# Halving the first layer norm's row sums, moving a later one to ScalarE, and cutting the last store in two on a kernel that keeps TensorE busy

## The chip, the cores and the metric

One core of a Trainium2 chip. The metric is the device time of one launch in microseconds (us). The kernel runs at the full granted TensorE clock (1.00). Below, PE is TensorE, DVE is VectorE, ACT is ScalarE, SP is SyncE; SPq and ACTq are the queues from which SyncE and ScalarE issue transfers.

## The reference, cut to what matters

Two layers, each an attention part A and a gated part B, on one sequence of 2048 tokens with 1024 features, in bf16:

```python
x = x + A(layernorm(x), wqkv, wo)      # qkv = ln @ wqkv; 32 heads; a window of 8 keys at stride 2; then @ wo
x = x + B(layernorm(x), w1, w3, w2)    # (silu(ln @ w1) * (ln @ w3)) @ w2, inner size 3584
x = x + A(layernorm(x), wqkv, wo)
x = x + B(layernorm(x), w1, w3, w2)
```

The layer norm has no learnt scale: (x - mean) / sqrt(var + 1e-5) for each token.

## The kernel before

The program is written as a list of operations with the keys that they read and write. A small scheduler in the kernel file then places them by modelled times and emits every engine's instructions in that order. So an edit of one operation can move instructions of other engines. Tokens are handled in four chunks of 512, each of four tiles of 128 tokens.

**The head.** To start matmuls early, the first two token tiles are only centred, not scaled. Their row sums are made like this: tile 0 by halves on two engines, tile 1 whole on ScalarE. PE transposes the centred tiles (through `ident`), the transposes are evacuated to `ce`, and PE multiplies them by the rows of the query weights as these rows land:

```python
dve(0.77, ... tensor_scalar(xn[2][:, 0:512], x_sb[0][:, 0:512], 1.0 / D, 0.0, ..., accum_out=mean[:, 0:1]), ...)
act(0.82, ... activation(xn[3][:, 0:512], x_sb[0][:, 512:1024], ACTF.Copy, scale=1.0 / D, accum_out=part[:, 0:1]), ...)
act(1.25, ... activation(xn[3][:], x_sb[1][:], ACTF.Copy, scale=1.0 / D, accum_out=mean[:, 1:2]), ...)
for j in range(2):
    for h in range(2):
        ... # dve: xn[j] half h = x_sb[j] half h - mean
    transposed(xn[j], ..., ce[:, :, j * P:(j + 1) * P], ..., pieces of the evacuation)
...
for kk, j0, j1 in [(k, j, j + 1) for j in range(2) for k in range(3)] + [(k, 0, 2) for k in range(3, KT)]:
    ...  # 8 matmuls: weight row kk times tiles j0 to j1; reads ("w", row kk) and ("ce", j, kk)
```

After these come 64 matmuls of 256 columns for tiles 2 and 3, and then the key product and everything else with 512 columns.

**The last chunk's layer norm** before its query, key and value products uses DVE's statistics instructions, two of 512 columns and one aggregate for each of the four tiles:

```python
for j in range(TPC):
    stats(j)
root(0, TPC)
```

**The tail.** The very last matmul group is 128 columns wide; DVE adds it to x and the result is stored from one queue:

```python
evac(dve, ..., tensor_tensor(xs, xs, bank[a.bank][:, 0:cn], op=ALU.add), ...)
if l == 1:
    dma(cn // 4, xout[:, n, hh * 512 + c0:hh * 512 + c0 + cn], xs, [("x", n, hh)], [("out", n, hh)], 0)
```

## Time and profile before

| | before |
|---|---|
| time, median of 5 runs | 1614.94 us (1614.66 to 1615.42) |
| span in the profiled run | 1613.1 us |
| PE / DVE / ACT busy | 1601.3 / 1122.3 / 329.6 us |
| start of the first 512-column matmul | 21.49 us |
| from there to the end of the last add | 1589.16 us |
| from the last add to the end of the span | 2.48 us |

The page of the kernel before: its span, the busy times with their shares and instruction counts, and the chain that ended last by engine.

```profile
span 1613.1 us, 19082 instructions
PE 1601.3 (99%) x7463; PEld 762.7 (47%) x7610; DVE 1122.3 (70%) x1906; ACT 329.6 (20%) x526; POOL 5.3 (0%) x28
PE 99%; issue 1%; DMA 0%; ACT 0%; DVE 0%; ACTq 0%
```

The Trainium skill ("Trainium Kernel Development and Optimization", Performance Expectations) warns that matmul busy time is a bad metric of how close a kernel is to its limit, because matmuls are pipelined. A busy share alone would not show where time can be gained, so look at the waits. The wait view of PE in the kernel before (engine and line, what it waited for, us in total, times, longest) lists these three and no more:

```profile
PE bank L285 <- PEq L757: 0.8, 1, 0.8
PE bank L430 <- DVE xn L472: 0.4, 1, 0.4
PE bank L521 <- DMA slot<-in_A_wqkv_dram: 0.2, 1, 0.2
```

All three lie before 7 us. Between 21.49 us and its last matmul PE waits for nothing that the view lists, and then only the last add follows: this stretch is 1589.16 us of matmuls. The windows view of exactly that stretch (us from the start, its length, busy us and instructions of each engine, granted clock, DMA share, GB/s):

```profile
21.49:1610.65 1589.16, 1581.09 (x7271) 746.74 (x7416) 1112.98 (x1878) 317.16 (x501) 0.00 (x0) 1.00 0.59 176
```

What can be gained is therefore in the first 21.5 us and the last 2.5. The timeline of PE at the head (start, duration, line, operation, count, and in brackets the idle time before it and what ended it):

```profile
5.19 0.61 PE L521 MATMUL bank<-hT,slot 128*128 128x128 bf16 x8
5.96 0.62 PE L521 MATMUL bank<-hT,slot 128*128 128x128 bf16 x8 [0.16 <-DMA slot<-in_A_wqkv_dram]
6.96 0.66 PE L430 MATMUL bank<-ident,xn 128*128 128x128 bf16 x8 [0.39 <-DVE xn L472]
7.46 5.44 PE L521 MATMUL bank<-hT,slot 128*128 128x128 bf16 x64
...
14.51 1.69 PE L535 MATMUL bank<-xnT,slot 128*128 128x256 bf16 x14
```

L521 is the product with the query weights (the first two lines are weight rows 0 and 1 for tile 0), the L430 line is the transposes of tile 1, and L535 begins the 256-column matmuls. PE stands idle 0.39 us until DVE has centred tile 1. What DVE waits for there, in the timeline of DVE and ACT:

```profile
5.37 1.06 ACT L460 ACTIVATE xn<-x 128x1024 bf16<-128x1024 bf16 x1 [1.35 <-DMA x<-in_A_x_dram]
6.33 0.19 ACT L460 ACTIVATION_READ_ACCUMULATOR xn<-x 128x1 f32 x1
6.55 0.62 DVE L472 TENSOR_SCALAR xn<-x,mean 128x512 bf16<-128x512 bf16 x2 [1.22 <-ACT xn L460]
```

The tail, in the timeline of the kernel before: the last add, and the issue of the last store.

```profile
1610.36 0.29 DVE L700 TENSOR_TENSOR x<-x,bank 128x128 bf16<-128x128 bf16 x1 [1.27 <-PE bank L347]
1610.68 0.33 SPq L261 DMA_DIRECT2D out_dram<-x  x1
```

### The profile page before, as it was taken

The page shows a single profiled execution, that of the slowest core. Times are in us where ns is not written, and L with a number is a line of the kernel's source. Part 1 is how long each engine was busy: PE and PEld are TensorE (multiplying, and loading weights), DVE is VectorE, ACT ScalarE, POOL GpSimd, SP SyncE. Part 2 cuts the span into 40 slices and gives each one's busy share as a digit, 9 for nine tenths or more (in the row PEclk, how much of TensorE's full clock was granted, in tenths as well). Part 3 has the DMA queues.
Part 4 walks back from the last instruction along what each step waited for, and adds up shares of the span by engine and source line. Part 5 has one row for each costly group of instructions (what it writes and reads, how often), then busy time and mean ns, then how long its engine had stood idle before and what let it go on. Part 6 is the DMA issues. An engine that isn't in the chain of part 4 may idle for free.

```text
span 1613.1 us, 19082 instructions
## 1 busy us (share of the span) xinstructions
PE 1601.3 (99%) x7463; PEld 762.7 (47%) x7610; DVE 1122.3 (70%) x1906; ACT 329.6 (20%) x526; POOL 5.3 (0%) x28
## 2 busy tenths in 40 slices
PE   9999999999999999999999999999999999999999
PEld 7555544444444444444444444444444444444444
DVE  5899888988889888898898729884299831211211
ACT  5423322021201222113311032110321101101110
POOL 1000000000000000000000000000000000000000
PEclk9999999999999999999999999999999999999999
DMA  9834755495548764858545487365873464454451
GB/s 321 228 105 151 221 166 171 127 227 158 171 141 253 194 186 137 216 164 251 176 131 163 157 248 228 121 176 174 254 220 118 160 179 156 144 177 149 156 167 42
DMA packets 350649, 285.80 MB, mean 177 GB/s; under 512 B 72288, under 2 KB 344928, under 8 KB 350560
## 3 DMA queue, kind: packets, MB, share of 16 engines
q1 hardware_dynamic: 350128, 283.94, 58.8%
q8 instruction: 59, 0.97, 0.2%
q10 hardware_dynamic: 432, 0.66, 0.1%
q14 instruction: 30, 0.25, 0.1%
HBM read 238.94 MB, written 29.36 MB: 166 GB/s over the span
## 4 chain that ended last, share of the span: by engine, by line
PE 99%; issue 1%; DMA 0%; ACT 0%; DVE 0%; ACTq 0%
PE bank L347 98%; PE bank L535 0%; PE bank L521 0%; DMA x<-in_A_x_dram 0%; PE bank L430 0%; ACT L281 0%; DVE xn L472 0%; ACT xn L460 0%; DVE x L700 0%; ACTq L460 0%
## 5 line engine op out<-in xcount | busy, mean ns | idle before, releaser
L347 PE MATMUL bank<-xnT,slot 128*128 128x512 bf16 x4955 | 1088.7, 379 | 5.3
L347 PEld LDWEIGHTS <-slot 128*128 128x128 bf16 x5056 | 518.2, 102 | 572.9
L347 PE MATMUL bank<-slot,hT 128*128 128x512 bf16 (+2 forms) x1812 | 387.3, 372 | 1.9
L670 DVE TENSOR_TENSOR hT<-sg,bank 128x512 bf16<-128x512 bf16 x224 | 153.4, 685 | 214.4 <-PE bank L347 194.9
L265 DVE TENSOR_TENSOR scr<-scr 128x1024 bf16<-128x1024 bf16 (+3 forms) x576 | 293.4, 539 | 2.0
L347 PEld LDWEIGHTS <-hT 128*128 128x128 bf16 x1848 | 178.5, 98 | 208.7
L668 ACT ACTIVATE sg<-bank 128x512 bf16<-128x512 f32 x224 | 133.7, 597 | 660.5 <-PE bank L347 608.8
L265 DVE TENSOR_TENSOR scr<-qT,kT 128x2048 bf16<-128x2048 bf16 x128 | 154.1, 1219 | 73.3 <-DMA kT<-qkv_d 71.0
L405 ACT CAST sgt<-bank 128x512 bf16<-128x512 f32 x184 | 107.3, 585 | 315.2 <-PE bank L347 300.3
L265 DVE TENSOR_TENSOR scr<-pA,vT 128x2048 bf16<-128x2048 bf16 x128 | 152.5, 1220 | 0.3
L700 DVE TENSOR_TENSOR x<-x,bank 128x512 bf16<-128x512 bf16 (+1 forms) x66 | 43.9, 670 | 121.5 <-PE bank L347 121.4
L347 PE MATMUL bank<-wo,oT 128*128 128x512 bf16 x502 | 112.6, 379 | 0.6
L313 DVE BATCH_NORM_STATS2 st<-x 128x6 f32<-128x512 bf16 x124 | 81.8, 681 | 11.9 <-DMA x<-in_A_x_dram 11.4
L347 PEld LDWEIGHTS <-oT 128*128 128x128 bf16 x512 | 50.1, 98 | 60.3
L645 DVE TENSOR_TENSOR x<-x,bank 128x512 bf16<-128x512 bf16 x64 | 43.9, 687 | 37.0 <-PE bank L347 35.8
L320 ACT ACTIVATE sd<-mv,epst 128x4 f32<-128x4 f32 (+1 forms) x17 | 5.1, 297 | 172.4 <-DVE mv L316 172.1
L628 DVE STREAM_TRANSPOSE pA<-pB 128x2048 bf16<-128x2048 bf16 x16 | 37.0, 2310 | 0.5
L605 DVE STREAM_TRANSPOSE pB<-pA 128x2048 bf16<-128x2048 bf16 x16 | 37.0, 2310 | 0.5
L668 ACT ACT_TABLE_LOAD x20 | 25.7, 1283 | 56.2 <-PE bank L347 56.0
L265 DVE TENSOR_TENSOR pA<-scr 128x256 bf16<-128x256 bf16 x128 | 35.9, 286 | 0.4
L265 DVE TENSOR_TENSOR oT<-scr 128x256 bf16<-128x256 bf16 x128 | 33.9, 288 | 0.1
L327 DVE TENSOR_SCALAR xn<-x,mv,rstd 128x1024 bf16<-128x1024 bf16 x62 | 30.7, 541 | 3.5 <-DMA xnT<-xn 3.4
(61 smaller groups left out, 209.0 us busy)
## 6 DMA issues: line engine op xcount, KB each, us to landing
slot<-in_B_w_dram SPq DMA_DIRECT2D x160, 1024.0 KB, 5.9
slot<-in_A_wqkv_dram SPq DMA_DIRECT2D x28, 1024.0 KB, 5.1
qkv_d<-sgt SPq DMA_DIRECT2D x92, 256.0 KB, 3.3
qT<-qkv_d SPq DMA_DIRECT2D x16, 512.0 KB, 5.7
slot<-in_B_w_dram SPq DMA_DIRECT2D x16, 512.0 KB, 5.7
kT<-qkv_d SPq DMA_DIRECT2D x14, 544.0 KB, 6.7
vT<-qkv_d SPq DMA_DIRECT2D x14, 544.0 KB, 4.9
out_dram<-x SPq DMA_DIRECT2D x31, 128.0 KB, 4.3
```

The costliest lines, as they stand in the source:

```text
L265: return lambda _: nc.vector.tensor_tensor(o, a, b, op=op)
L313: dve(0.67, lambda _, hh=hh: nc.vector.bn_stats(st[q][:, j, hh, :], x_sb[n][:, hh * 512:(hh + 1) * 512]), [("x", n, hh)] + list(after), [( ...
L320: act(0.3, lambda _: nc.scalar.activation(sd[q][:, j0:j1], mv[q][:, j0:j1, 1], ACTF.Sqrt, bias=epst[:]), [("mv", q, j) for j in range(j0, ...
L327: dve(0.5, lambda _: nc.vector.tensor_scalar(xn[j][:], x_sb[n][:], mv[q][:, j, 0:1], rstd[q][:, j:j + 1], op0=ALU.subtract, op1=ALU.mult), ...
L347: nc.tensor.matmul(bank[a.bank][:, 0:ncol], lhsT=w, rhs=r, start=first and i == 0, stop=last and i == n - 1)
L405: evac(act, 0.59, lambda _, a=a, i=i, m=m: nc.scalar.copy(sgt[i][:, m % 2, :], bank[a.bank][:]), op, [], [("sgt", i, m % 2)], a)
L605: dve(2.31, lambda _: nc.vector.transpose(psmT[:].rearrange("p c d -> p (c d)"), psm[:].rearrange("p w s -> p (w s)")), allA, ["pB"])
L628: dve(2.31, lambda _: nc.vector.transpose(At[:].rearrange("p w s -> p (w s)"), AeT[:].rearrange("p c d -> p (c d)")), ["pB"], allA)
L645: evac(dve, t1(512), lambda _, xs=xs, a=a: nc.vector.tensor_tensor(xs, xs, bank[a.bank][:], op=ALU.add), op, [("x", n, hh)], [("x", n, hh) ...
L668: evac(act, 0.6, lambda _, i=i, a=ag: nc.scalar.activation(sg[i][:], bank[a.bank][:], ACTF.Silu), og, [], [("sg", i)], ag, table="silu")
L670: evac(dve, t1(512), lambda _, i=i, a=au, f=f: nc.vector.tensor_tensor(hT[:, f, :], sg[i][:], bank[a.bank][:], op=ALU.mult), ou, [("sg", i ...
L700: evac(dve, t1(cn), lambda _, xs=xs, a=a, cn=cn: nc.vector.tensor_tensor(xs, xs, bank[a.bank][:, 0:cn], op=ALU.add), op, [("x", n, hh)], [ ...
```

## The change

The intent is to shorten both ends. Tile 1's row sum is made by halves on two engines as tile 0's is; its sum of squares moves behind the evacuations on ScalarE; the last chunk's sums go to ScalarE, which has more room than DVE; the output weights `wo` come in four loads, not five; and the last store leaves as two halves of 64 partitions (rows), on two queues at once.

```diff
+        def sums(j):      # Copy with scale 1/D, then Square with bias mean, scale -1, each with accum_out
+            act(1.25, ... ACTF.Copy, scale=1.0 / D, accum_out=mv[q][:, j, 0:1] ...)
+            act(1.35, ... ACTF.Square, bias=mv[q][:, j, 0:1], scale=-1.0, accum_out=mv[q][:, j, 1:2] ...)
...
-            stats(j)
-        root(0, TPC)
+            if on_act:    # l == 0 and c == NCH - 1
+                sums(j)
+            else:
+                stats(j)
+        root(0, TPC, D if on_act else 1)
...
-        act(1.25, lambda _: nc.scalar.activation(xn[3][:], x_sb[1][:], ACTF.Copy, scale=1.0 / D,
-                                                 accum_out=mean[:, 1:2]), ...)
         for j in range(2):
+            dve(0.77, ... xn[2][:, 0:512], x_sb[j][:, 0:512] ... accum_out=mean[:, j:j + 1]),
+                [("x", j, 0)] + [("ce", 0, 2)] * j, ...)
+            act(0.82, ... xn[3][:, 0:512], x_sb[j][:, 512:1024] ... accum_out=part[:, j:j + 1]), ...)
...
-                       ((0, 2, "DVE"), (2, 4, "DVE"), (4, 8, "ACT")) if j == 0 else ((0, 4, "DVE"), (4, 8, "ACT")))
+                       ((0, 2, "DVE"), (2, 4, "DVE"), (4, 8, "ACT")))
...
-                [("x", j, 0), ("x", j, 1), ("mean", j)] + [("ce", 1, KT - 1)],
+                [("x", j, 0), ("x", j, 1), ("mean", j), ("xnT", b, 3, 1) if j else ("ce", 1, KT - 1)],
...
-        for t0, t1_ in ((0, 2), (2, 4), (4, 6), (6, 7), (7, 8)):
+        for t0, t1_ in ((0, 2), (2, 4), (4, 6), (6, 8)):
...
-                    dma(cn // 4, xout[:, n, hh * 512 + c0:hh * 512 + c0 + cn], xs, [("x", n, hh)], [("out", n, hh)], 0)
+                    parts = ((0, 64, "SP"), (64, P, "AQ")) if pi == len(pieces) - 1 and tail else ((0, P, "SP"),)
+                    for p0, p1, queue in parts:
+                        dma(cn * (p1 - p0) // 512, xout[p0:p1, n, hh * 512 + c0:hh * 512 + c0 + cn], xs[p0:p1],
+                            [("x", n, hh)], [("out", n, hh, p0)], 0, queue=queue)
```

Because the scheduler sees other durations, PE's order changed too: weight row 2's eight matmuls for tile 0 now stand before the transposes of tile 1 instead of after them. I call these the new and the old order.

More of the change, by code (lines that the diff above doesn't have):

```diff
@@ L302, with ln @@
     stage_no = [0]
-    def ln(c, first=False):
+    def ln(c, first=False, on_act=False):
         s = stage_no[0]
@@ L317, in stats, with root @@
                 [("st", q, j, 0), ("st", q, j, 1)], [("mv", q, j)], pri)
-        def root(j0, j1):
-            act(0.3, lambda _: nc.scalar.activation(sd[q][:, j0:j1], mv[q][:, j0:j1, 1], ACTF.Sqrt, bias=epst[:]),
+        def sums(j):
+            xt = x_sb[c * TPC + j]
+            keys = [("x", c * TPC + j, hh) for hh in range(2)]
+            act(1.25, lambda _: nc.scalar.activation(xn[j][:], xt[:], ACTF.Copy, scale=1.0 / D,
+                                                     accum_out=mv[q][:, j, 0:1]), keys, [("xn", j), ("mv", q, j)], 1)
+            act(1.35, lambda _: nc.scalar.activation(xn[j][:], xt[:], ACTF.Square, bias=mv[q][:, j, 0:1], scale=-1.0,
+                                                     accum_out=mv[q][:, j, 1:2]), keys, [("xn", j), ("mv", q, j)], 1)
+        def root(j0, j1, n=1):
+            act(0.3, lambda _: nc.scalar.activation(sd[q][:, j0:j1], mv[q][:, j0:j1, 1], ACTF.Sqrt, bias=epst[:],
+                                                    scale=1.0 / n),
                 [("mv", q, j) for j in range(j0, j1)] + ["eps"], [("sd", q, j) for j in range(j0, j1)], -9 if first else 0, table="sqrt")
@@ L413, in q_stage @@
     def q_stage(l, c):
-        b = ln(c)
+        b = ln(c, on_act=l == 0 and c == NCH - 1)
         for which in range(3):
@@ L453, in q_first @@
         ce = hT[:, 8:16, :]
-        dve(0.77, lambda _: nc.vector.tensor_scalar(xn[2][:, 0:512], x_sb[0][:, 0:512], 1.0 / D, 0.0, op0=ALU.mult,
-                                                    op1=ALU.add, accum_out=mean[:, 0:1]),
-            [("x", 0, 0)], [("xn", 2), ("mean", 0)], -9)
-        act(0.82, lambda _: nc.scalar.activation(xn[3][:, 0:512], x_sb[0][:, 512:1024], ACTF.Copy, scale=1.0 / D,
-                                                 accum_out=part[:, 0:1]), [("x", 0, 1)], [("xn", 3), ("part", 0)], -9)
@@ L459, in q_first @@
-        rows[2](6, queue="AQ", after=[("part", 0)])
-        act(1.25, lambda _: nc.scalar.activation(xn[3][:], x_sb[1][:], ACTF.Copy, scale=1.0 / D,
-                                                 accum_out=mean[:, 1:2]), [("x", 1, 0), ("x", 1, 1)],
-            [("xn", 3), ("mean", 1)], -9)
-        for j in range(2):
-            for h in range(2):
-                c0 = 512 * h
-                if j == 0:
-                    dve(0.31, lambda _, c0=c0: nc.vector.tensor_scalar(
-                        xn[0][:, c0:c0 + 512], x_sb[0][:, c0:c0 + 512], mean[:, 0:1], part[:, 0:1], op0=ALU.subtract,
-                        op1=ALU.subtract), [("x", 0, 0), ("x", 0, 1), ("mean", 0), ("part", 0)],
-                        [("xn", 0), ("xn", 0, h)], -9)
-                else:
-                    dve(0.31, lambda _, c0=c0: nc.vector.tensor_scalar(
-                        xn[1][:, c0:c0 + 512], x_sb[1][:, c0:c0 + 512], mean[:, 1:2], None, op0=ALU.subtract),
-                        [("x", 1, 0), ("x", 1, 1), ("mean", 1)], [("xn", 1), ("xn", 1, h)], -9)
+        for j in range(2):
+            dve(0.77, lambda _, j=j: nc.vector.tensor_scalar(xn[2][:, 0:512], x_sb[j][:, 0:512], 1.0 / D, 0.0,
+                                                             op0=ALU.mult, op1=ALU.add, accum_out=mean[:, j:j + 1]),
+                [("x", j, 0)] + [("ce", 0, 2)] * j, [("xn", 2), ("mean", j)], -9)
+            act(0.82, lambda _, j=j: nc.scalar.activation(xn[3][:, 0:512], x_sb[j][:, 512:1024], ACTF.Copy,
+                                                          scale=1.0 / D, accum_out=part[:, j:j + 1]),
+                [("x", j, 1)], [("xn", 3), ("part", j)], -9)
+            if j == 0:
+                rows[2](6, queue="AQ", after=[("part", 0)])
+            for h in range(2):
+                dve(0.31, lambda _, j=j, c0=512 * h: nc.vector.tensor_scalar(
+                    xn[j][:, c0:c0 + 512], x_sb[j][:, c0:c0 + 512], mean[:, j:j + 1], part[:, j:j + 1],
+                    op0=ALU.subtract, op1=ALU.subtract), [("x", j, 0), ("x", j, 1), ("mean", j), ("part", j)],
+                    [("xn", j), ("xn", j, h)], -9)
@@ L475, in q_first @@
             transposed(xn[j], [("xn", j, h) for h in range(2)], ce[:, :, j * P:(j + 1) * P],
                        [("ce", j, k) for k in range(KT)],
-                       ((0, 2, "DVE"), (2, 4, "DVE"), (4, 8, "ACT")) if j == 0 else ((0, 4, "DVE"), (4, 8, "ACT")))
-        dve(0.16, lambda _: nc.vector.tensor_tensor(mean[:, 0:1], mean[:, 0:1], part[:, 0:1], op=ALU.add),
-            [("mean", 0), ("part", 0), ("ce", 1, 0)], [("mean", 0)], -9)
+                       ((0, 2, "DVE"), (2, 4, "DVE"), (4, 8, "ACT")))
@@ L480, in q_first @@
+        dve(0.16, lambda _: nc.vector.tensor_tensor(mean[:], mean[:], part[:], op=ALU.add),
+            [("mean", j) for j in range(2)] + [("part", j) for j in range(2)] + [("ce", 1, 0)],
+            [("mean", j) for j in range(2)], -9)
         for j in range(2, TPC):
@@ L642, in t_stage @@
                 op = mm8(a, [(oT[oh][:, t, j * P:(j + 1) * P], wo[:, t, hh * 512:(hh + 1) * 512]) for t in range(KT)],
-                         True, True, [("oT", oh, t) for t in range(KT)] + [("wo", t) for t in (0, 2, 4, 6, 7)], lane=1)
+                         True, True, [("oT", oh, t) for t in range(KT)] + [("wo", t) for t in (0, 2, 4, 6)], lane=1)
                 xs = x_sb[n][:, hh * 512:(hh + 1) * 512]
```

## The prediction

> **What bounds the kernel.** TensorE. The page gives PE 1601.3 us busy of a 1613.1 us span, at full granted clock; the chain of waits is 99% PE. Matmuls run every 0.216 us (the chain's pieces, 49 in 10.74 us; the 0.05 us breaks between pieces look like lost records). The wait view gives PE three short waits after its warm-up, all before 7 us, and none until its last matmul at 1610.34. So only the first 22 us and the last 2.8 us can give anything; DVE (70% busy) and ScalarE (20%) are off the path. The Trainium skill warns ("Trainium Kernel Development and Optimization", Performance Expectations) that matmul busy time is a bad metric; I rely on the constant interval and the missing waits.
>
> **What the change moves.**
>
> 1. *Token tile 1 by halves.* Before (timeline): x tile 1 lands at 5.33; ScalarE sums its 1024 columns in 1.06 + 0.19 us; DVE subtracts from 6.55; PE starts the transposes at 6.96. After: two 512-column sums side by side (DVE 0.61 + 0.08, ScalarE 0.63 + 0.19) make the centred tile ready about 0.3 us earlier. But the instruction order shows PE doing weight row 2's eight matmuls for tile 0 before these transposes, and row 2 lands at about 6.6. PE then transposes from about 7.1 and starts tile 1's products at about 7.65 instead of 8.06: 0.4 us. The gain then shrinks: DVE now writes normalised tile 0 (0.53 us) before it evacuates the transposes of tiles 2 and 3, so the 256-column matmuls that began at 14.67 begin at about 14.4. Weight rows land just in time (row 5 about 10.7).
> 2. *Tile 1's squares later on ScalarE* (1.15 + 0.19 us). Its DMA transpose is issued at about 17.3 instead of 14.9; undisturbed ones of this trace land in 3.1 to 3.4 us, so at 20.6, before the K products need it at 21.2. Tight; I expect no stall.
> 3. *Last chunk's sums on ScalarE.* About 6.3 us off DVE (eight statistics of 0.68, four aggregates of 0.2), about 10.3 us onto ScalarE. Neither is on the path: 0.
> 4. *wo in four loads, not five*: 0.
> 5. *Last store.* Before: last add ends 1610.65, issue 0.33 us, packets 1611.56 to 1611.83, landed 1612.17, closing barrier to 1613.1. Issue took 0.33 us for 128 rows of 256 or 512 bytes alike, so half the rows hardly shorten it. The skill ("DMA: Bandwidth & Descriptors", Issuing engines are not separate DMA queues) says several issuers share the same 16 engines and save only issue time. Gain 0 to 0.1.
>
> **Sum.** About 0.25 us at the head and 0.05 at the tail: 1614.94 becomes 1614.6 us. The 8-in-10 range is 1614.0 to 1615.3, as the runs before already spread over 0.6. Chances: faster by over 2% 0.003, within 2% 0.99, slower by over 2% 0.007.
>
> **What would show it.** Timeline: tile 1's transposes at about 7.1, its first products at 7.65, the 256-column matmuls about 0.25 us earlier. Waits: PE on weight row 2 near 6.5, none at the K products. ScalarE busy about 10 us up, DVE 6 us down, PE unchanged. Last matmul to end: 2.7 to 2.8 us.
>
> **What would make it wrong.** Tile 1's transpose landing after 21.2: PE would wait up to 1 us. Weight rows or later loads landing later. A weight or spill transfer that the new order puts behind something late. A second queue at the end that has to be waited for longer than one.

## The result, and the profile after

1615.57 us median of 5 runs (1615.36 to 1616.06) against 1614.94. That is 0.63 us more where 0.34 less was predicted, and outside the stated range. The ratio of the two is 1.0004 (95% interval 0.999 to 1.0017). Ratios here are the mean time of one kernel's fast runs over that of the other's fast runs of the same rounds, so they are not quite the ratio of the medians that I quote. The effect is far below the 2% at which a verdict is "faster" or "slower", and 1 lies within the interval, so by whole times alone the two kernels are the same. I read the difference all the same because the runs repeat within a few tenths, no run of the changed kernel was as fast as the median before, and the parts of the span can be read one by one.

The page of the changed kernel, the same lines:

```profile
span 1613.6 us, 19080 instructions
PE 1601.2 (99%) x7463; PEld 762.7 (47%) x7610; DVE 1116.8 (69%) x1897; ACT 336.4 (21%) x541; POOL 5.0 (0%) x28
PE 99%; issue 1%; DMA 0%; SPq 0%; DVE 0%
```

DVE lost 5.5 us and ScalarE got 6.8 us. The middle did not feel it. The windows view of the changed kernel from its first 512-column matmul to the end of its last add:

```profile
21.42:1610.58 1589.16, 1581.09 (x7271) 746.72 (x7416) 1106.95 (x1866) 324.42 (x516) 0.00 (x0) 1.00 0.58 176
```

The same 1589.16 us, and it is the same in the traced runs of all kernels. So every span is a head, 1589.16, and a tail.

The tail, in the timeline of the changed kernel:

```profile
1610.29 0.29 DVE L706 TENSOR_TENSOR x<-x,bank 128x128 bf16<-128x128 bf16 x1 [1.28 <-PE bank L359]
1610.61 0.56 SPq L261 DMA_DIRECT2D out_dram<-x  x1
1610.62 0.57 ACTq L257 DMA_DIRECT2D out_dram<-x  x1
```

Two issues start within 0.01 us of each other, and each takes 0.56 us where the whole store took 0.33. The transfers view of the same stretch (KB each, us from issue to landing), where the kernel before had 32.0 KB and 1.4:

```profile
out_dram<-x SPq DMA_DIRECT2D x1, 16.0 KB, 1.8
out_dram<-x ACTq DMA_DIRECT2D x1, 16.0 KB, 2.1
```

The packet records say more (us after the end of the last add; "landed" is the last of a transfer's 16 semaphore updates; "closing" is from the last landing to the end of the span):

```
               first packet   last packet ends   landed   closing
before  SPq        0.86             1.12          1.47      1.02
after   SPq        1.23             1.47          1.83
        ACTq       1.51             1.74          2.09      0.89
```

So the last landing came 0.63 us later; the closing sequence of the program was 0.13 shorter (see the last section); the head of the profiled run was 0.07 shorter. That makes -0.07 + 0.63 - 0.13 = +0.43, the difference of the two spans (1613.57 and 1613.14). The 0.63 has two parts: the first half landed 0.36 later than the whole store had (1.83 against 1.47), and the second half another 0.27 later, for its packets began only after the first half's.

The head, in the timeline of PE of the changed kernel:

```profile
5.49 1.05 PE L527 MATMUL bank<-hT,slot 128*128 128x128 bf16 x16
6.73 0.62 PE L527 MATMUL bank<-hT,slot 128*128 128x128 bf16 x8 [0.19 <-DMA slot<-in_A_wqkv_dram]
7.18 0.61 PE L442 MATMUL bank<-ident,xn 128*128 128x128 bf16 x8
7.84 4.99 PE L527 MATMUL bank<-hT,slot 128*128 128x128 bf16 x56
...
14.44 1.80 PE L541 MATMUL bank<-xnT,slot 128*128 128x256 bf16 x15
```

PE now waits for a DMA, weight row 2, before it transposes tile 1 (L442); and the products of tile 1 (7.84) follow only after a break: the last transpose started at 7.57, and nothing is left to do while the transposes are evacuated. (The durations in this view are modelled, so the 7.18 + 0.61 of the line hides the break; the starts show it.) And DVE and ACT, in the timeline of the changed kernel:

```profile
5.01 0.63 ACT L470 ACTIVATE xn<-x 128x512 bf16<-128x512 bf16 x1 [0.69 <-DMA x<-in_A_x_dram]
5.14 0.49 DVE L447 COPY hT<-bank 128x256 bf16<-128x256 bf16 x2
5.54 0.68 DVE L467 TENSOR_SCALAR_CACHE_REDUCE xn<-x 128x512 bf16<-128x512 bf16 x1
6.34 0.74 DVE L476 TENSOR_SCALAR xn<-x,mean,part 128x512 bf16<-128x512 bf16 x2
```

Tile 1 had landed at 4.92 and ScalarE took its half at once, but DVE was still evacuating tile 0's transposes and began its half at 5.54.

### The profile page after: what moved, and what is told of

Its sections match the earlier page's. It is cut to its first block, busy times and chain, and to the rows that moved or that the text cites. A ratio compares the mean times of both kernels' runs of the same rounds, so it can differ in the third digit from the quotient of the medians.

```text
span 1613.6 us, 19080 instructions
## 1 busy us (share of the span) xinstructions
PE 1601.2 (99%) x7463; PEld 762.7 (47%) x7610; DVE 1116.8 (69%) x1897; ACT 336.4 (21%) x541; POOL 5.0 (0%) x28
## 4 chain that ended last, share of the span: by engine, by line
PE 99%; issue 1%; DMA 0%; SPq 0%; DVE 0%
PE bank L359 98%; PE bank L541 0%; PE bank L527 0%; DMA slot<-in_A_wqkv_dram 0%; SPq L261 0%; PE bank L442 0%; DVE hT L447 0%; DVE x L706 0%
## 5 line engine op out<-in xcount | busy, mean ns | idle before, releaser
L313 DVE BATCH_NORM_STATS2 st<-x 128x6 f32<-128x512 bf16 x116 | 76.9, 682 | 10.1 <-DMA x<-in_A_x_dram 9.7
```

What stands on the lines that cost most here:

```text
L313: dve(0.67, lambda _, hh=hh: nc.vector.bn_stats(st[q][:, j, hh, :], x_sb[n][:, hh * 512:(hh + 1) * 512]), [("x", n, hh)] + list(after), [( ...
```

## The experiments

The theories. A: two issues at the same moment slow each other. Rivals in the tail: B, a store of 64 rows is slow by itself; C, ScalarE's queue is slow after long idleness; R, the loss is elsewhere. H, for the head: the new order ties tile 1 to the landing of weight row 2. L, its rival: the loads bind the head whatever the order. The jobs ran on different chips. "Before" was run again in every job, and every difference below is against its median of the same rounds. Differences of up to about 0.3 us can be noise (see the check at the end of "What binds the head").

### First job: the tail (before 1615.02)

**t1_split_only**: the kernel before with only the store's part of the diff, `((0, 64, "SP"), (64, P, "AQ"))`.

> The kernel before, with only the last store split over two queues. Theory A (two issues started in the same 10 ns slow each other): the tail alone costs the loss, so slower than before by 0.4 to 0.65 us, both issues about 0.56 us instead of 0.33, packets of the two queues one after the other, last landing about 2.1 us after the last add instead of 1.47. Rival R (the loss is not in the tail's split but in the head or in later loads): within 0.15 us of before.

Measured 1615.69 us, +0.67. The split alone costs all that the change cost, so R fell. The timeline of t1_split_only:

```profile
1610.80 0.55 SPq L261 DMA_DIRECT2D out_dram<-x  x1
1610.81 0.56 ACTq L257 DMA_DIRECT2D out_dram<-x  x1
```

The last landing came 2.07 us after the last add.

**t2_both_sp**: the same two halves from one queue.

```diff
-((0, 64, "SP"), (64, P, "AQ"))
+((0, 64, "SP"), (64, P, "SP"))
```

> The same two halves of the rows, both issued by SyncE one after the other. Theory A: each issue takes about 0.33 us, the second half starts about 0.4 us after the first and lands 0.3 to 0.45 us later than the whole store did; slower than before by 0.3 to 0.45 us. Rival B (a store of 64 rows is slow by itself): each issue takes about 0.56 us and the loss is 0.6 us or more.

Measured 1615.93 us, +0.91. The timeline of t2_both_sp:

```profile
1610.76 1.18 SPq L261 DMA_DIRECT2D out_dram<-x  x2
```

Two issues, one after the other, of 0.55 and 0.58 us by the trace, and the first packet 1.22 us after the add. Nothing ran beside the first issue, and it was just as slow. Theory A fell as the cause of the slow issue, and B held its ground. That the second half's packets came after the first's (0.27 us of the 0.63) is a part that this run does not test.

**t3_whole_aq**: the whole store of 128 rows from ScalarE's queue, `((0, P, "AQ"),)`.

> The whole last store, 128 rows, from ScalarE's queue, which has been idle since 4 us. Theory A: one issuer, so 0.33 us of issue and about 1.47 us from the last add to the landing; within 0.15 us of before. Rival C (the ScalarE queue is slow to start after long idleness): issue about 0.56 us and 0.3 to 0.6 us slower.

Measured 1615.20 us, +0.18: 0.03 outside theory A's band and below C's, with runs from 1614.74 to 1615.24. In its profile the issue took 0.35 us and the landing came 1.51 us after the add, against 1.47. So C is not the cause. Where the +0.18 lay is not settled: its profiled run was its fastest, and the closing was there 0.18 us shorter than before (0.84), not longer.

**h1_no_split**: the changed kernel with the store whole again, `((0, P, "SP"),)`.

> The changed kernel with the last store whole again, so the head, the sums on ScalarE and the wo loads remain. Theory A with the head gain read from the profiles (256-column matmuls 0.07 us earlier): 0.0 to 0.2 us faster than before. Rival R: still slower than before by about 0.5 us.

Measured 1615.16 us, +0.14: the loss of the tail is gone, but there is no gain. Its landing is as before (1.48), its closing 0.12 shorter. PE's timeline in h1_no_split shows what its head waited for in that run:

```profile
7.15 0.62 PE L527 MATMUL bank<-hT,slot 128*128 128x128 bf16 x8 [0.66 <-DMA slot<-in_A_wqkv_dram]
7.61 0.61 PE L442 MATMUL bank<-ident,xn 128*128 128x128 bf16 x8
```

In this run row 2 landed at 7.10 us, 0.4 later than in the changed kernel's run, and PE waited for it.

### Second job: the head and the middle (before 1615.27)

**h2_order**: h1_no_split with the old order, pinned by a key that only the scheduler sees.

```diff
-                    [("xn", j), ("xn", j, h)], -9)
+                    [("xn", j), ("xn", j, h), ("xc", j, h)], -9)
...
-                        [lk[0][1]] + [("ce", j, kk) for j in range(j0, j1)], [], ...)
+                        [lk[0][1]] + [("ce", j, kk) for j in range(j0, j1)] + [("xc", 1, 1)] * ((kk, j0) == (2, 0)), ...)
```

> h1_no_split with PE's order at the head put back: tile 1's transposes before weight row 2's matmuls for tile 0, which then hide the evacuation of the transposes. Theory H (the new order ties tile 1 to the landing of weight row 2, and leaves PE waiting 0.2 us for the evacuation): 256-column matmuls 0.1 to 0.4 us earlier than in h1_no_split (its 14.86), no PE wait on a weight row of over 0.3 us before the transposes, and 0.1 to 0.3 us faster than h1_no_split. Rival L (the head is bound by the landing of the loads themselves, whatever the order): within 0.1 us of h1_no_split.

Measured 1615.43 us, +0.16, so no better against its own rounds than h1_no_split (+0.14). As a test it is spoilt: the pin also moved the transposes of tiles 2 and 3 apart in PE's order, and PE then waited 0.2 us for tile 2. The 512-column matmuls began at 22.11 in its profile.

**h4_swap_after** and **h5_swap_before**: weight rows 2 and 3 exchanged in the load order, in h1_no_split and in the kernel before. PE's order stayed the same in both; only the landing of row 2 moved.

```diff
-        for kk in range(4):
+        for kk in (0, 1, 3, 2):
             rows[2](kk)
```

> h1_no_split with the loads of weight rows 2 and 3 exchanged, so that row 2 lands about 0.66 us later; PE's order unchanged (new order). Theory H: PE waits about 0.6 us longer for row 2 before tile 1's transposes, and the kernel is 0.4 to 0.7 us slower than h1_no_split. Rival L: within 0.15 us of h1_no_split.

> The kernel before with the same exchange of rows 2 and 3; PE's order unchanged (old order: tile 1's transposes first). Theory H: row 2 lands at about 7.2, just before its matmuls at 7.4, so within 0.2 us of before. Rival L: the same loss as in h4_swap_after.

h4_swap_after: 1615.83 us, +0.56, which is 0.42 more than h1_no_split's +0.14; PE's wait grew by 0.40 us, not the 0.6 expected. h5_swap_before: 1615.27 us, +0.00. The timelines of PE, first h4_swap_after:

```profile
8.23 0.62 PE L527 MATMUL bank<-hT,slot 128*128 128x128 bf16 x8 [1.06 <-DMA slot<-in_A_wqkv_dram]
```

and h5_swap_before:

```profile
7.47 0.66 PE L430 MATMUL bank<-ident,xn 128*128 128x128 bf16 x8 [0.47 <-DVE xn L472]
7.97 5.44 PE L521 MATMUL bank<-hT,slot 128*128 128x128 bf16 x64
```

The new order waits for row 2 with everything else behind it; the old order transposes meanwhile and does not feel the same delay (row 2 landed at 7.63, before its matmuls began at 7.97). This pair holds for H and against L.

**h3_sums_wo**: the kernel before with only the last chunk's sums on ScalarE and the four wo loads.

> The kernel before with only the last chunk's sums on ScalarE and four wo loads. Every theory: DVE busy 5 to 6.5 us less, ScalarE 8 to 10.5 us more, no new PE wait, time within 0.15 us of before. If it is slower by over 0.2 us, a stall sits in the middle of the kernel.

Measured 1615.68 us, +0.41: the expectation of +/-0.15 failed. But there was no stall in the middle: 1589.16 us again, no PE wait after 6 us. Over the whole page DVE was busy 6.0 us less (1116.3) and ScalarE 9.3 more (338.9), as expected. The landing came at 1.48. What was longer is the closing sequence, 1.33 us instead of 1.02 (see the last section): 0.32 of the 0.41.

### Third job: what of the store is slow (before 1615.26)

**t4_cols**: two halves of the columns, 128 rows each, on two queues at once.

```diff
+                    for d0, d1, queue in ((0, 64, "SP"), (64, cn, "AQ")) if last else ((0, cn, "SP"),):
+                        dma((d1 - d0) // 4, xout[:, n, hh * 512 + c0 + d0:hh * 512 + c0 + d1], xs[:, d0:d1], ...)
```

> The kernel before, last store split into two halves of the columns (128 rows of 128 bytes each), one on each queue. Theory B2 (after t2_both_sp: what is slow is a store of fewer than 128 rows, on whatever queue): both issues about 0.33 to 0.36 us, first packets at about 0.86 us after the last add, 0 to 0.35 us slower than before. Rival A2 (any two stores issued at once slow each other): both issues about 0.56 us and 0.5 us or more slower.

Measured 1615.19 us, -0.07. Timeline of t4_cols:

```profile
1610.81 0.33 SPq L261 DMA_DIRECT2D out_dram<-x  x1
1610.82 0.37 ACTq L257 DMA_DIRECT2D out_dram<-x  x1
```

Two queues at once are not slow by themselves. The packets of the two overlapped (0.86 to 1.10 and 0.94 to 1.18 us after the add), the last landing came at 1.61 instead of 1.47.

**t5_rows**: a look. Three earlier stores of the last tile, which nobody waits for, cut by rows.

```diff
+                    cuts = {0: (0, 64, P), 1: (0, 32, P), 2: (0, 96, 112, P)}.get(pi, (0, P)) if tail else (0, P)
+                    for p0, p1 in zip(cuts, cuts[1:]):
```

> A look only: three of the last tile's earlier stores, which nobody waits for, cut by rows into 64+64, 32+96 and 96+16+16 of 1024 bytes, on one queue. Theory B2: the stores of 64, 32 and 16 rows take about 0.55 us of issue or more, the whole ones 0.33 us; 96 rows tell whether the rule is the row count or its being 128. Rival: only the final 256-byte halves were slow, and these take 0.33 us. No effect on the time beyond 0.3 us, as 6 us lie between these stores.

The timeline of t5_rows; the first two are the 64-row halves, then 32 rows, then 96:

```profile
1593.23 0.55 SPq L261 DMA_DIRECT2D out_dram<-x  x1
1593.83 0.58 SPq L261 DMA_DIRECT2D out_dram<-x  x1
1599.27 0.35 SPq L261 DMA_DIRECT2D out_dram<-x  x1
1605.31 0.32 SPq L261 DMA_DIRECT2D out_dram<-x  x1
```

Of the counts tried, only 64 rows are slow. Stores of fewer rows (16, 32) and of 96 are not, so "fewer than 128", as I had written, fell too. The one run took 1615.83 us, 0.57 more than before and beyond the 0.3 expected; its closing was 1.47 us (0.46 longer), its landing 1.48.

**h6_halves_old_order** and **h7_halves_new_order**: the kernel before with only tile 1's halves, with the pin of h2_order and without it.

> The kernel before with only tile 1's halves, PE's order pinned to the old one (tile 1's transposes before weight row 2). Theory H2 (the head runs into whichever load lands last: tile 1, weight row 2, tile 3): 0 to 0.3 us faster than before and 0.1 to 0.4 us faster than h7_halves_new_order; in its profile the 512-column matmuls begin less than 16.2 us after tile 1's landing. Rival L (no order helps): within 0.1 us of h7.

> The same without the pin: the order that the change as handed in got. Theory H2: in its profile the 512-column matmuls begin 14.7 to 14.8 us after weight row 2's landing, as in the changed kernel (14.74), h1_no_split (14.75) and h4_swap_after (14.77); time within 0.3 us of before, on the slow side: 0 to 0.3 us slower.

h6: 1615.13 us, -0.13. h7: 1615.82 us, +0.56. So with the same halves the two orders differ by 0.69 us, more than expected. In h7 a second loss joined the wait for row 2: DVE put two other tiles' scaling before an evacuation. PE's timeline in h7_halves_new_order shows PE waiting for that evacuation at the end of the head:

```profile
14.37 0.61 PE L430 MATMUL bank<-ident,xn 128*128 128x128 bf16 x8
15.39 0.82 PE L530 MATMUL bank<-xnT,slot 128*128 128x256 bf16 x6 [0.41 <-DVE xnT L435]
```

So this pair shows that the new order costs, but not how much of it is the wait for row 2. Two of the expectations failed: in h6 the 512-column matmuls began 16.36 us after tile 1's landing and not less than 16.2, and in h7 15.3 and not 14.7 to 14.8 us after row 2's. The 0.41 us wait of h7 is absent in the changed kernel, where tile 1's squares come later; so I take it that this part of the change does its work when tile 1 goes by halves in the new order; no run changes it alone.

### Fourth job: the count of 64, and the best version again (before 1615.21)

**t6_96_32**: t1_split_only cut at another row.

```diff
-((0, 64, "SP"), (64, P, "AQ"))
+((0, 96, "SP"), (96, P, "AQ"))
```

> t1_split_only with the last store cut into 96 and 32 rows instead of 64 and 64, still two queues at once. Theory B3 (after t5_rows, where 16, 32 and 96 rows were issued in 0.32 to 0.42 us and 64 rows in 0.55 to 0.58: only the count of 64 is slow): issues 0.32 to 0.42 us, last landing 1.45 to 1.75 us after the last add instead of 2.07, within 0.25 us of before. Rival (row halves on two queues cost by themselves, whatever their count): 0.45 us or more slower, as t1_split_only was (0.67).

Measured 1615.25 us, +0.04, against +0.67 for 64 and 64. Timeline of t6_96_32:

```profile
1610.78 0.35 SPq L261 DMA_DIRECT2D out_dram<-x  x1
1610.78 0.38 ACTq L257 DMA_DIRECT2D out_dram<-x  x1
```

The packets of both queues overlap (0.87 to 1.15 and 0.97 to 1.19 us after the add), and the last landing is at 1.66.

**t8_rows2**: another look, `{0: (0, 32, 96, P), 1: (0, 48, P), 2: (0, 112, P)}`.

> A look only, as t5_rows, with rows 32+64+32, 48+80 and 112+16. Theory B3: the 64 rows in the middle (from row 32) take about 0.55 us of issue, every other count 0.32 to 0.42 us. Rival (what is slow is a cut at row 64, not the count): all of them 0.32 to 0.42 us.

All cuts of the two looks, from the trace (rows of 1024 bytes; us of issue; us from issue to landing; a second or third store of a group stands behind the first in the queue):

```
rows           issue         landing        place in its group
16             0.41-0.42     1.50-1.65      second or third
32             0.34-0.36     1.49-1.50      first
32             0.58          1.72           third, right behind 64 rows
48             0.32          1.57           first
64             0.55          2.02           first  (rows 0 to 63)
64             0.58          2.03           second (rows 64 to 127)
64             0.62          1.95           second (rows 32 to 95)
80             0.42          1.72           second
96             0.32          1.67           first
96             0.41          1.84           second
112            0.32          1.85           first
128            0.33-0.36     1.69-1.74      whole
```

The place of the cut does not matter: the 64 rows in the middle are as slow as the others. A store of 32 rows right behind one of 64 is slow as well (0.58 against the 0.41 to 0.42 of other seconds and thirds); B3 had not expected that, and I read it as waiting behind the slow one, which no run tests. The one time was 1615.56 us, with a closing of 1.48.

**h6_again**: h6_halves_old_order once more.

> The same kernel as h6_halves_old_order, once more, to see whether the best version is really ahead of before: 0.05 to 0.25 us faster than before if so; rival: within 0.05 us of before or slower.

Measured 1615.18 us, -0.03: the rival's band. With -0.13 from the first time, the version is at best 0.1 us ahead of before, and its runs (1614.85 to 1615.62 in both jobs) overlap those of before. I do not claim that it beats it. No version here clearly does.

### What binds the head

The landings in the profiled runs (us; "landed" as above), the start of DVE's subtraction for tile 1, and the start of the 512-column matmuls:

```
                      tile 0,        tile 1   row 2    subtract   512 columns
                      second half    landed   landed   starts     start
before                   3.27         5.28     6.56      6.55       21.49
h3_sums_wo               3.99         5.34     6.69      6.61       21.55
h5_swap_before           3.50         5.79     7.63      7.06       22.00
h6_halves_old_order      3.58         5.06     6.52      6.36       21.42
after                    3.57         4.92     6.68      6.34       21.42
h1_no_split              3.52         5.12     7.10      6.29       21.85
h4_swap_after            3.58         5.00     8.18      6.66       22.92
```

Three readings. In the first three, which have the tile-1 sum whole, the subtraction starts 1.27 us after tile 1's landing, to the digit, and the 512 columns 16.21 us after it. With halves it starts 1.17 to 1.66 us after it (last four; 1.41 to 1.53 in h2_order, h7 and h6_again, which the table leaves out), so it is mostly later, and in h1 0.10 earlier: DVE's half stands behind the evacuation of tile 0. In h6, after and h1 it starts 2.77 to 2.78 us after the landing of tile 0's second half, which is what that evacuation depends on. And in the new order (last three) the 512 columns start 14.74 to 14.75 us after row 2's landing: that is now what the head waits for. In the other seven traced runs with the tile-1 sum whole the 1.27 us hold as well, but the 512 columns start 16.27 to 16.61 us after tile 1's landing; in six of these seven they start 11.26 to 11.28 us after tile 3's, which looks like one more limit close by. The landings themselves move by some tenths from launch to launch, so these differences, not the starts alone, are to be compared.

How far can a head be read from a median? Six kernels have the head's code of before (t1, t2, t3, t4, t6 and h3). Take the change of their tail in the trace from the change of their median, and -0.20 (t4_cols) to +0.32 us (t3_whole_aq) is left, though nothing in their heads was edited. So a remainder of 0.3 us is noise or moving landings. The same subtraction gives +0.25 for h1_no_split, which is inside that scatter, and +0.67 for h4_swap_after and +0.55 for h7, which are outside it.

## Why the prediction was wrong, point by point

- *What bounds the kernel*: right. PE does the same 1589.16 us between the same two points in all kernels.
- *Step 5, last store, "half the rows hardly shorten it ... Gain 0 to 0.1"*: this is the step that failed. It measured as a loss of 0.63 us at the landing in the profile, and as a loss of 0.67 alone (t1_split_only). The estimate took the 0.33 us of issue from stores of 128 rows and carried it over to 64 rows, a shape that the trace before does not contain. Stores of 64 rows take 0.55 to 0.62 us of issue, and at the tail the first packet left about 0.37 us later; the second half then landed 0.27 us after the first. Why the halves of 64 rows queue up like this, when those of t4_cols and t6_96_32 overlap, is open. The guess among the risks, "a second queue at the end that has to be waited for longer than one", named the place but not the cause: the second queue alone costs 0.14 to 0.19 us at the landing (t4_cols, t6_96_32), and next to nothing in time.
- *Step 1, "make the centred tile ready about 0.3 us earlier"*: this failed too, at no cost that can be told from noise. The term took both half sums to begin at tile 1's landing. DVE's began behind tile 0's evacuation, and the subtraction started 1.42 us after the landing in the changed kernel, against 1.27.
- *Step 1, "starts tile 1's products at about 7.65 instead of 8.06: 0.4 us"*: mis-read on both sides. I took 8.06 from the chain, whose matmul ends are modelled. By their starts, the matmuls after the transposes begin at 7.46 in the trace before and come every 0.056 us, so tile 1's, after the first eight, begin at about 7.91. After the change they begin at 7.84, as PE has nothing to do while the transposes are evacuated (0.27 us from the last transpose's start). What remains is the 0.07 us of the profiled run, and nothing in the medians: h1_no_split is 0.14 us slower than before although its closing is 0.12 shorter. That would make its head some 0.26 us longer, which the scatter above does not tell from noise. What is shown is that the head of the new order follows row 2's landing (14.74 to 14.75 us in three traces) and loses when row 2 is late (the pair h4 and h5).
- *Step 2, the later transposing transfer*: right. It was issued at 17.0 us and landed at 20.1; the key product began at 21.42 without a wait.
- *Steps 3 and 4*: right in time as far as PE shows (no wait, 1589.16). DVE -5.5 us as said (6); ScalarE +6.8, not 10. Part of that miss is the number of times that ScalarE loads a table of functions (ACT_TABLE_LOAD, 1.28 us each): 46 before, 45 after, and 47 in h3_sums_wo, which got 9.3.
- *Sum*: predicted -0.3, measured +0.63. In the profiled runs the sum is head -0.07, landing +0.63, closing -0.13. The other 0.2 us of the median lies in runs that were not traced; since the middle is constant, it may lie in the head, but it is inside the scatter and not shown.

## What to carry to other kernels

Before cutting a transfer, time the exact shape that the cut will give it, in a place where nobody waits: one look with several cuts told here what two theories had missed. Where a scheduler orders the instructions, look at what the edit put in front of what, and ask which load the first engine now waits for; a faster sum was worth nothing once PE stood behind a weight row. And when one engine is constant over the middle of the kernel, cut the span into head, middle and tail and compare each, for effects of a few tenths of a us drown in the whole.

## What the Trainium skill lacked or had wrong

- "DMA: Bandwidth & Descriptors", Rules for kernel authors, says of two transfers to disjoint partition halves "Don't bother — they serialize" and to use one transfer of 128 partitions. I had not drawn on that row. The advice holds here (64 and 64 rows: +0.67 us, packets of the two queues one after the other). But it cannot be the whole reason that both halves use the same DMA engines, as the row says: 96 and 32 rows on two queues, each with 16 semaphore updates too, overlapped and cost +0.04 us, while two stores of 64 rows from one queue took 0.55 and 0.58 us of issue.
- The same page, no section: that a store of 64 rows is slow to issue, 0.55 to 0.62 us, against 0.32 to 0.42 for 16, 48, 80, 96, 112 and 128 rows and for 32 rows not behind a 64-row one. What in the issue makes it so stays open.
- The same page, Issuing engines are not separate DMA queues, says that a second issuer only saves issue time. The runs agree: two column halves at once (t4_cols) gained nothing at the landing, which came 0.14 us later than that of one whole store.
- No page that I read says that the closing of a program differs between kernels. From the last landing to the end of the span it takes 0.84 to 1.48 us here, the same to 0.01 us where a kernel (or its near twin) was traced twice (h6 and h6_again, t5 and t8): 1.02 in before, 0.89 in the changed kernel, 1.33 in h3_sums_wo. The traces differ in SyncE's last two DRAIN instructions: in before the second begins 0.36 us after the instruction in front of it, in h3_sums_wo the first 0.33 us, where the changed kernel shows 0.07 and 0.05. Why is open. At this scale it is as large as the effects studied.
